# q of batches 5 to 7 transposed by DMA out of zero-padded token rows in SBUF; batch 0's last V product in other banks; a new order of steps

## The chip, the core and the metric

The kernel runs on one core of a Trainium2 chip. The metric is device time in microseconds (us) for one execution; lower is better. Engines are named as in the profile: PE multiplies matrices (PEld is its weight load), DVE is the vector engine, ACT the scalar engine, POOL issues the casting loads from DRAM and does a few copies, and SP issues the transposing DMAs and the stores.

## What is computed

Sliding-window attention over 8 batches, 8 heads, 576 positions and 64 channels, and behind it a two-layer network with the activation h - tanh(h):

```python
scores = scale * np.matmul(q, k.transpose(0, 1, 3, 2))      # q, k, v: (8, 8, 576, 64), scale = 1/8
mask = (rel >= 0) & (rel < 64)                              # rel = query position - key position
attn = softmax(where(mask, scores, -1e9))
x = (attn @ v) as 4608 tokens x 512
h = x @ w_in                                                # 512 -> 2048
out = (h - tanh(h)) @ w_out                                 # 2048 -> 512
```

## The kernel before

Everything is bf16 on PE with float32 accumulation. The kernel schedules nothing by itself: one long list of steps, `PLAN`, is played from left to right, each word is a step with its arguments, and each step puts its instructions at the end of its engines' queues. So the order within each engine is the order of the list, and an engine that waits holds up all that stands behind it.

**Attention.** Heads are taken in pairs; pair g = 4*batch + pr holds heads pr and pr+4, so that two heads share 128 partitions. A batch has nine windows of 64 queries. `Rp.g.i.bank` multiplies three windows of a pair (keys times zero-padded queries, line 300), `Rx` is their exp on ACT (line 305), `M.g` the mask multiply on DVE (line 393), `PP.g` the product with V for the two pairs g and g+1 (36 matmuls, line 418), `DR` and `DN` its normalization on DVE (lines 426 to 438) into `xs`, and `Y.b` two transposing DMAs on SP that carry a batch's `xs` into the token chunks `xT` (line 472). The first three batches reach `xT` by PE transposes instead (`Xp`, line 453, and the copies `Xc`). Batch 0 is done head by head, with `P.g` (line 405) and `D.g` (lines 445 to 447) for one pair at a time.

**How k and q reach their layouts.** For the early batches POOL loads rows with a cast (`lk`, `lq`, `LQ`, lines 108 and 114), DVE or ACT copies them into pair order (`ck`, `cq`), PE transposes them six pieces at a time (`Fp`, `Ep`, line 261), and ACT or DVE copies the result out of PSUM (`Fc`; `Ea` and `Eb` for the two halves of q, which leave the other half zero). From batch 3 on, k comes another way: `lr.b.i.h` (line 176) loads 128 tokens of four heads as rows of 64 numbers into a token-major tile, and `tk.b.i` (line 181) is a DMA transpose on SP from that tile into `kw`. For batches 6 and 7, q takes a third way: `LQ.b` loads the batch, `cz.g` (line 128, POOL) spreads a pair into the zeroed tile `qz`, `bo.g` (line 133, SP) writes that to DRAM, and `td.g` (line 138, SP) reads it back with a DMA transpose into `qT`, of which there are two (`NR = 2`).

**The network.** Tokens come in nine chunks of 512 columns. `H.c.m` is one block of 128 hidden units for chunk c (four matmuls 512 columns wide, line 487), `A.c.m` its tanh on ACT (line 495), `G.c.m` the subtraction on DVE (line 501), `W.c.s.part` four of the sixteen matmuls that make 128 output rows (line 526), and `O.c.s` the copy out of PSUM and the store (line 542). The last 128 rows of the last chunk are made in two column halves (line 519), `W.8.3.0` and `W.8.3.1` for half 0, `W.8.3.2` and `W.8.3.3` for half 1, with the stores `O.8.3` and `O.9.0` (line 537). `H` writes banks `(m + c) % 3` in chunks 0 and 1, and `m % 2` later; a bank is free again when its `G` has read it.

The weights are loaded by POOL: `wi.0`, `wi.1` and `wi.2` (line 189) hold hidden blocks 0 to 3, 4 to 7 and 8 to 15; `wo.0` to `wo.3` (line 197) hold the second layer. `U.n` are matmuls on a zero tile that only keep PE running. `z` clears the `qz` tiles (line 235). `LV`, `lv`, `lt` load V, and `Z.b`, `za`, `zb` copy V between partition halves.

## Time and profile before

| what | value |
|---|---|
| three runs | 313.97, 315.15 and 315.36 us, median 315.15 us |
| the profiled execution | 314.95 us, of which its instructions span 313.3 us |
| PE clock granted | 0.998 of full over the span |
| DMA issues by line 176, 160, 108 and 114 on POOL | 50, 35, 22 and 5 |
| DMA transposes on SP, lines 181, 138 and 472 | 25, 8 and 10 |
| DVE busy from 60 to 80 us | 18.02 of 20 us |
| last POOL instruction | before 200 us |

Rows of the groups give: line, engine, operation, tiles written<-read, shapes, how often | busy us, mean ns of one | idle us of the engine ahead of them, and what ended it. A mean for a matmul of 512 columns is 379 ns because neighbours overlap in the pipeline; what counts is how far apart their starts are, which the chain of waits shows (eight in 1.73 us). The chain's rows are: start in us, length in us, what, how many. The timeline's rows are: start, length, engine, line, operation, tiles, how many, and in brackets idle time of the engine ahead of it and who ended it.

### The profile page before, as it was taken

The numbers are of one execution on the slowest core, as the hardware profiler recorded it, in microseconds if no ns is written. First come the engines' busy times: TensorE is split into PE (matmuls) and PEld (weight loads), VectorE is DVE, ScalarE is ACT, GpSimd is POOL, SyncE is SP. The second block draws the span as 40 slices with busy tenths as digits, with TensorE's granted clock in tenths as the row PEclk, the third lists the DMA queues.
The fourth block names the chain that finished last, engine by engine and source line by source line (L and its number), as shares of the span: only waits on it lengthen the run. The fifth ranks groups of instructions, "written<-read, shape, count | busy, mean of one in ns | idle before, by whom it ended". The sixth has DMA issues, their size and how long they took to land.

```text
span 313.3 us, 6081 instructions
## 1 busy us (share of the span) xinstructions
PE 302.4 (97%) x2385; PEld 165.0 (53%) x2413; DVE 187.8 (60%) x327; ACT 171.2 (55%) x320; POOL 108.6 (35%) x160
## 2 busy tenths in 40 slices
PE   6988999999999999999999999999999999999995
PEld 2564565656655555555555455555554444444444
DVE  3685988699758785667556555873774534343300
ACT  3576875489866767657454536445333533433311
POOL 8990666686739442293441640000000000000000
PEclk9999999999999999999999999999999999999999
DMA  9999999999999999997999999481005110010111
GB/s 158 149 181 203 170 208 137 192 138 141 142 116 151 143 156 159 127 132 170 175 183 165 181 193 175 113 180 36 35 36 116 59 37 33 33 37 33 67 69 67
DMA packets 113133, 39.11 MB, mean 125 GB/s; under 512 B 96336, under 2 KB 107600, under 8 KB 113104
## 3 DMA queue, kind: packets, MB, share of 16 engines
q0 software_dynamic: 72064, 18.06, 67.1%
q1 hardware_dynamic: 41040, 20.65, 30.5%
q8 instruction: 19, 0.31, 0.4%
q14 instruction: 10, 0.08, 0.1%
HBM read 36.70 MB, written 11.80 MB: 155 GB/s over the span
## 4 chain that ended last, share of the span: by engine, by line
PE 87%; DMA 5%; POOL 5%; issue 1%; ACT 0%; POOLq 0%; ACTq 0%
PE ps L487 39%; PE ps L526 37%; PE ps L300 4%; PE ps L418 3%; DMA xT<-xs 3%; DMA wi<-in_moe_w_in_dram 3%; PE ps L261 2%; POOL kall L108 1%; POOL vw L160 1%; POOL qall L108 1%; PE ps L519 1%; PE ps L453 1%; POOL vw L147 0%; POOL seen L241 0%; ACT ysb L88 0%
## 5 line engine op out<-in xcount | busy, mean ns | idle before, releaser
L501 DVE TENSOR_TENSOR gT<-ps,th 128x512 bf16<-128x512 f32 x144 | 97.3, 687 | 81.9 <-ACT th L495 81.2
L487 PE MATMUL ps<-xT,wi 128*128 128x512 bf16 x576 | 141.7, 379 | 1.1 <-DMA wi<-in_moe_w_in_dram 0.7
L526 PE MATMUL ps<-w_out_sb,gT 128*128 128x512 bf16 x532 | 131.8, 379 | 1.4
L495 ACT ACTIVATE th<-ps 128x512 f32<-128x512 f32 x144 | 84.6, 597 | 77.8 <-PE ps L487 75.6
L487 PEld LDWEIGHTS <-wi 128*128 128x128 bf16 x576 | 62.0, 113 | 50.4 <-DMA wi<-in_moe_w_in_dram 0.9
L526 PEld LDWEIGHTS <-gT 128*128 128x128 bf16 x560 | 53.0, 98 | 56.9
L305 ACT ACTIVATE pt<-ps 128x384 bf16<-128x384 f32 (+2 forms) x92 | 45.8, 504 | 20.3 <-PE ps L300 19.0
L176 POOL DMA_DIRECT2D kall<-in_k_dram x50 | 37.2, 758 | 28.2 <-DMA kw<-kall 19.9
L160 POOL DMA_DIRECT2D vw<-in_v_dram x35 | 31.1, 894 | 10.8 <-PE ps L418 8.6
L88 ACT ACTIVATE ysb<-ps 128x512 f32<-128x512 f32 (+1 forms) x23 | 13.3, 579 | 28.4 <-PE ps L526 25.9
L393 DVE TENSOR_TENSOR pt<-pt,ps 128x1152 bf16<-128x1152 bf16 x28 | 20.6, 745 | 2.7 <-ACT pt L305 2.7
L300 PEld LDWEIGHTS <-kw 128*128 128x128 bf16 x180 | 14.4, 98 | 11.7 <-issue 0.3
L88 ACT ACTIVATE qt<-ps 64x576 bf16<-64x576 bf16 x30 | 19.3, 642 | 1.3 <-PE ps L300 0.3
L300 PE MATMUL ps<-qt,kw 128*128 128x128 bf16 x180 | 19.0, 219 | 0.0
L128 POOL COPY qz<-qall 96x384 bf16<-96x384 bf16 x16 | 7.6, 528 | 24.9 <-DMA qd<-qz 11.6
L438 DVE TENSOR_TENSOR xs<-ps,rcp 128x384 bf16<-128x384 f32 x28 | 14.9, 548 | 0.1
L225 PE MATMUL ps<-warm 128*128 128x512 bf16 x26 | 9.3, 496 | 2.2 <-DVE warm L206 2.1
L90 DVE COPY ysb<-ps 128x512 f32<-128x512 f32 x14 | 9.6, 685 | 3.1 <-PE ps L526 3.1
L418 PEld LDWEIGHTS <-pt 128*64 128x64 bf16 x504 | 9.2, 112 | 3.0 <-issue 1.3
L418 PE MATMUL ps<-vw,pt 128*64 128x65 bf16 x504 | 10.7, 197 | 0.0
L261 PE MATMUL ps<-ident,qb 96*128 96x96 bf16 x132 | 9.3, 206 | 1.0 <-DVE qb L90 1.0
L261 PEld LDWEIGHTS <-qb 96*128 96x128 bf16 x132 | 7.5, 97 | 4.5 <-DVE qb L90 1.9
(69 smaller groups left out, 165.4 us busy)
## 6 DMA issues: line engine op xcount, KB each, us to landing
out_dram<-ysb SPq DMA_DIRECT2D x35, 256.0 KB, 2.2
vw<-in_v_dram POOLq DMA_DIRECT2D x28, 128.0 KB, 5.3
qall<-in_q_dram POOLq DMA_DIRECT2D x5, 576.0 KB, 8.7
kall<-in_k_dram POOLq DMA_DIRECT2D x40, 64.0 KB, 4.8
qd<-qz SPq DMA_DIRECT2D x8, 288.0 KB, 3.3
w_out_sb<-in_moe_w_out_dram POOLq DMA_DIRECT2D x4, 512.0 KB, 8.4
kall<-in_k_dram POOLq DMA_DIRECT2D x11, 144.0 KB, 4.7
qall<-in_q_dram POOLq DMA_DIRECT2D x11, 144.0 KB, 4.6
```

Source lines behind the costliest of these rows:

```text
L88: nc.scalar.activation(o, i, ACT.Copy)
L160: nc.gpsimd.dma_start(out=w[:, 2 * i + 1, :, 0:D] if i < NF else w[64:128, 2 * i, :, 0:D], in_=v[b, :, 128 * i:128 * i + n].rearrange("h p ...
L176: nc.gpsimd.dma_start(out=token_rows(b)[0:c, i, :, h, :], in_=k[b, NP * h:NP * h + NP, 128 * i:128 * i + c].rearrange("r p d -> p r d"))
L261: nc.tensor.transpose(tp[:, e, :], src[:, e, :], ident[:P, :P])
L300: nc.tensor.matmul(sp[:, i], kt[:, 64 * j:64 * j + 128], qT[g % NR][:, :, 64 * j:64 * j + 64], start=first, stop=first or i == n - 1)
L305: nc.scalar.activation(PT[g % NPT][:, js[0]:js[0] + len(js), :].rearrange("p i (h t) -> p i h t", h=2), sp, ACT.Exp, scale=scale)
L393: nc.vector.tensor_tensor(p, p, mask.unsqueeze(1).to_broadcast([128, 2 * NJ, 64]), ALU.mult)
L418: nc.tensor.matmul(ps[r, bank, 65 * i:65 * i + 65], PT[(g + r2) % NPT][:, j, r], vw[b % 2][:, j, p0 + r2 + NP * h, :], start=True, stop=True)
L487: nc.tensor.matmul(hp, w_in_tile(ki, m), chunk_tile(c)[:, n.start // 64:n.stop // 64, ki % 2, 64 * (ki // 2):64 * (ki // 2) + 64], start=( ...
L495: nc.scalar.activation(th[:, n], hp, ACT.Tanh)
L501: nc.vector.tensor_tensor(gT[c][:, m, columns(s)], hp, th, ALU.subtract)
L526: nc.tensor.matmul(yp, gT[c][:, m, s * 128:(s + 1) * 128], w_out_sb[:, m, :], start=n == 1 and i == 0, stop=n == 4 and i == 3)
```

## The change

1. Batches 5, 6 and 7 get q in token rows. `Lq.b.half.i` on POOL loads 128 tokens (64 in the last) of four heads into the tile `q_rows`, where the other 64 columns of each head are zero; `tq.b.two.i` on SP transposes two pairs of these 128 tokens straight from SBUF into `qT`. There are 30 of each. `LQ.5` to `LQ.7`, all eight `cz`, `bo` and `td`, and the tiles `qz` and the DRAM buffer go away. So do the PE transposes of batch 5's q with their copies (`cq`, `Ep`, `Ea` and `Eb` of pairs 20 to 23).
2. `qT` has four pair slots in one tile instead of two tiles, so that `mq` clears four.
3. `z` clears `q_rows` (128 partitions of 5120 numbers) in one instruction, and stands in the list behind batch 1's last `Xc` instead of at the start.
4. Batch 0's last product with V (pair 2) goes to banks 0 and 1 instead of 5 and 6, and its normalization is cut into `DS.2` and two `DH.2`.
5. The last 128 output rows are cut at column 384: half 0 is the last 128 columns and half 1 the first 384.
6. The whole list of steps is in a new order. The end of it now ends `W.8.3.1`, `W.8.3.3`, `O.8.3`, `O.9.0` (before: `W.8.3.0`, `W.8.3.1`, `O.9.0`, `O.8.3`). The `U` matmuls are 26 before and 23 after; all of the 23 stand ahead of the first `H`.

```diff
-    qT = [const.tile([128, 2, S], BF16, name=f"qt{i}") for i in range(NR)]
+    q_two = const.tile([128, NP, 2, S], BF16, name="qt0")
+    qT = [q_two[:, i] for i in range(NP)]
+    q_rows = const.tile([128, NF + 1, NP, 2, 128], BF16, name="qr0")
-    qz = [const.tile([P, 2, E, 128], BF16, name=f"qz{i}") for i in range(2)]
...
-    def cast_q(g):
-
-        i = stage.pop((g, "q")).rearrange("p h (e d) -> p h e d", d=D)
-        for h in range(2):
-            nc.gpsimd.tensor_copy(qz[g % 2][:, h, :, 64 * h:64 * h + 64], i[:, h])
-
-    def bounce(g):
-
-        t = dram.tile([2, S, 128], BF16, tag="q", name="qd")
-        nc.sync.dma_start(out=t.rearrange("h (p e) c -> p h (e c)", e=E),
-                          in_=qz[g % 2].rearrange("p h e c -> p h (e c)"))
-        rows[g, "qd"] = t
-
-    def tr_dma(g):
-        nc.sync.dma_start(out=qT[g % NR].rearrange("c h s -> c (h s)"),
-                          in_=rows.pop((g, "qd")).rearrange("h s c -> (h s) c"), transpose=True)
+    def load_q_rows(b, half, i):
+
+        c = min(128, S - 128 * i)
+        nc.gpsimd.dma_start(out=q_rows[0:c, i, :, half, 64 * half:64 * half + 64],
+                            in_=q[b, NP * half:NP * half + NP, 128 * i:128 * i + c].rearrange("r p d -> p r d"))
+
+    def tr_q(b, two, i):
+
+        c = min(128, S - 128 * i)
+        nc.sync.dma_start(out=q_two[:, 2 * two:2 * two + 2, :, 128 * i:128 * i + c].rearrange("p r h c -> p (r h) c"),
+                          in_=q_rows[0:c, i, 2 * two:2 * two + 2].rearrange("p r h d -> p (r h d)"), transpose=True)
...
-    def more_zeros(i):
-        nc.vector.memset(qz[i], 0.0)
+    def more_zeros():
+        nc.vector.memset(q_rows, 0.0)
...
     def pv_banks(g):
-        return ps[:, 4:8:3, :] if g < NP and g % 2 and not BY_HEAD else ps[:, 5:7, :]
+        return ps[:, 0:2, :] if g == 2 else ps[:, 5:7, :]
...
+    def norm_sums(g):
+        ov = pv_banks(g)[:, :, 0:5 * (D + 1)].rearrange("p n (i c) -> p n i c", c=D + 1)
+        last[g] = sm_pool.tile([128, 2, 5, 1], F32, tag="rc", name="rc")
+        nc.vector.reciprocal(last[g], ov[:, :, :, D:D + 1])
+
+    def norm_half(g, n):
+        b, pr = divmod(g, NP)
+        k = 5 - n
+        ov = pv_banks(g)[:, n, 0:k * (D + 1)].rearrange("p (i c) -> p i c", c=D + 1)
+        nc.vector.tensor_tensor(xs[b % 2][:, 5 * n:5 * n + k, pr, :], ov[:, :, 0:D],
+                                last[g][:, n, 0:k].to_broadcast([128, k, D]), ALU.mult)
...
+    def last_columns(half):
+        n = 3 * d_model // 4
+        return slice(0, n) if half else slice(n, d_model)
```

Of the new order, the stretches that the prediction speaks of (loads and the first chunk; the end of chunk 0; the end of the list):

```diff
-    ... lq.4.p lk.4.p ... lq.7.p ... lv.1.1.1 P.3 wi.0 Eb.5.3.v wi.1 ... wi.2 ... lq.6.p ...
+    ... lq.7.p ... lk.4.p ... wi.0 ... ck.4.v P.3 D.3 ... Fp.4.3 P.2 DS.2 ... lk.7.p lk.6.p Xp.0.0.0.3 wi.1 DH.2.0 DH.2.1 ... lq.8.p Xc.0.1.0.3.v wi.2 ...
-    ... Xp.1.1.1.3 W.0.3.3 Xc.1.1.1.3.v Rx.9.1.4 Rp.8.1.4 O.0.2.a cq.10.a Ep.10.3 H.1.0 O.0.3.v ... G.1.0 ...
+    ... Xc.1.1.1.3.v z Ep.10.3 ck.10.v W.0.3.3 lr.5.2.1 Z.2 Rx.9.1.4 Rp.8.1.4 H.1.0 ... H.1.1 Fp.10.3 H.1.2 Rp.9.0.4 A.1.0 M.8 ... G.1.0 ... G.1.1 Fp.11.3 ... H.1.3 ...
-    ... W.8.2.3 W.8.3.2 O.8.1.a W.8.3.3 O.8.2.a W.8.3.0 W.8.3.1 O.9.0.a O.8.3.a
+    ... W.8.3.0 W.8.2.3 W.8.3.2 O.8.2.a W.8.3.1 W.8.3.3 O.8.3.a O.9.0.a
```

## The prediction

> **What bounds the kernel now.** I read the groups first, then the chain of waits, then the timeline at both ends.

> ```profile
> PE 302.4 (97%) x2385; PEld 165.0 (53%) x2413; DVE 187.8 (60%) x327; ACT 171.2 (55%) x320; POOL 108.6 (35%) x160
> ...
> L487 PE MATMUL ps<-xT,wi 128*128 128x512 bf16 x576 | 141.7, 379 | 1.1 <-DMA wi<-in_moe_w_in_dram 0.7
> L526 PE MATMUL ps<-w_out_sb,gT 128*128 128x512 bf16 x532 | 131.8, 379 | 1.4
> ```

> PE waits in all 2.5 us for its two large groups. The chain of waits tells when it begins and whether it ever stops:

> ```profile
> 17.52 8.44 DMA wi<-in_moe_w_in_dram
> 26.00 2.78 PE ps L487 x12
> ...
> 33.94 2.59 PE ps L487 x12
> ...
> 109.42 8.67 DMA xT<-xs
> ...
> 257.06 3.45 PE ps L526 x16
> ...
> 306.27 3.51 PE ps L519 x32
> ```

> Sixteen matmuls of 512 columns take 3.45 us, 0.216 us each. From the first of the network's matmuls at 26.00 us to the last at 309.8 us the PE's own work adds up, by such rows, to 282 us of the 283.8: 576 and 560 (weight loads; 28 matmul records are missing) x 0.216, line 519's 3.5, 243 score matmuls x 0.056, 504 V matmuls x 0.0215, 150 transposes x 0.043, 36 x 0.056. So after 26 us PE is full, and the time is: start of the first `H`, plus PE's work behind it, plus what PE is made to wait, plus the tail. The start and the tail:

> ```profile
> 25.01 0.56 DVE L90 COPY xT<-ps 128x512 bf16<-128x512 bf16 x2 [0.84 <-PE ps L453]
> ...
> 26.00 2.78 PE L487 MATMUL ps<-xT,wi 128*128 128x512 bf16 x12 [0.72 <-DMA wi<-in_moe_w_in_dram]
> ```

> ```profile
> 308.51 2.08 SPq L537 DMA_DIRECT2D out_dram<-ysb  x2
> 309.85 0.38 ACT L88 ACTIVATE ysb<-ps 128x256 f32<-128x256 f32 x1 [1.36 <-PE ps L519]
> ```

> The first `H` waits for `wi.0`; the last copy into `xT` was done 0.43 us sooner, at 25.57. Behind the last matmul come a copy of 256 columns and one store. The profiled execution took 314.95 us for a span of 313.3, 0.20 below the median of 315.15; the sum is made against 314.95.

> **PE's work behind the first H: -1.35 us.** Batch 5's q loses four `Ep`, each six transposes in 0.26 us (chain rows of line 261): -1.04. One warm-up matmul that stood near 76 us: -0.22. `Ep.4` moves ahead of the first `H` (-0.26), one score group moves behind it (+0.17). The copies that go with them (ten-odd on ACT and DVE of 0.35 to 0.83 us) and POOL's sixteen `cz` of 0.53 us lay beside full PE, so they are worth nothing.

> **First H: 0 (bounds -0.4 and +0.7).** POOL issues without a pause from 1.37 to 17.52 us, and 19 loads and the building of `ident`, `hide` and `seen` stand ahead of `wi.0` before and after, so `wi.0` goes at 17.5 and lands at 26.0 again. Batch 0's new banks save the last product its wait for the normalization before it, but `lk.4` is now the 19th load instead of the 18th, issued at 16.9 and landed some 4.5 us later (line 108's loads: 4.6 and 4.7 median), and `ck.4` on DVE waits for it ahead of `D.3`, `DS.2`, `DH.2` and three `Xc`: 21.6 + 0.4 + 1.05 + 0.2 + 0.9 + 1.5 = 25.65. The gain end is the copies' 25.57; the loss end a `lk.4` that takes the longest 5.3.

> **Wait for wi.2: +0.8 (0 to 1.4).** The three `wi` were issued back to back; the third, at 19.05, landed after 14.4 us (longest of its rows), at 33.5, and block 8, which needs it, began at 33.94, so the cover is 0.4. Now `lk.7`, `lk.6` and `lq.8` go between. Second and third landed at 28.5 and 33.5: 1024 KB in 5.0 us, so three loads of 144 KB push `wi.2` by 3 x 0.7 to 35.6. PE's work between first `H` and block 8 is eight blocks of 0.864, four score groups of 0.17, two `Fp` and the mask: 8.2, hence 34.2. I take the middle.

> **z in the full stretch of DVE: +0.8 (0 to 1.3).** Before, `z` was two clears at 3 us, where DVE had nothing. Now one of 2560 words stands at 60 us, where the windows view shows DVE at 18.02 of 20 us:

> ```profile
> 60.00:80.00 20.00, 19.96 (x189) 12.34 (x188) 18.02 (x32) 17.73 (x36) 13.65 (x19) 1.00 1.84 143
> ```

> Price: 768 words took 0.698 us and 576 words 0.538, 0.83 ns a word, so 2560 take 2.2 us. DVE then has `z` 2.2, `ck.10` 0.35, `Z.2` 1.49, `M.8` 0.74, and only then `G.1.0` 0.69. `Xc.1.1.1` ends at about 60.0, so `G.1.0` ends at 65.5. `H.1.3` needs its bank and would start at 64.6 (same count of PE's work). `H.1.0`'s start depends on none of it. What waits behind `H.1.3` is all of PE.

> **Tail: +0.35 (0.1 to 0.4).** PE's last two groups are the same columns. The last copy is 384 columns, between 0.38 (256) and 0.60 (512), so 0.49; the last store 192 KB, between 1.7 (128 KB) and 2.2 (256 KB). +0.11 and +0.25.

> **The new way of q: 0 (0 to +5).** POOL gives three `LQ` of 0.8 and sixteen `cz` back (10.9 us) and takes 30 `Lq` of 0.76 (22.8): it is done before 200 us in 108.6 us of work, so 12 more fit. SP gives eight `bo` of 0.53 and eight `td` of 1.28 back (14.5 us) and takes 30 transposes at `tk`'s median of 1.22 (37). That is cover that can run out, below. The transposes themselves move as much for batches 6 and 7 as before; batch 5 adds ten. The loads differ: 128-byte rows instead of 768.

> ```profile
> vw<-in_v_dram POOLq DMA_DIRECT2D x28, 128.0 KB, 5.3
> qall<-in_q_dram POOLq DMA_DIRECT2D x5, 576.0 KB, 8.7
> kall<-in_k_dram POOLq DMA_DIRECT2D x40, 64.0 KB, 4.8
> ...
> qall<-in_q_dram POOLq DMA_DIRECT2D x11, 144.0 KB, 4.6
> ```

> From 64 to 128 KB in short rows the landing grows by 0.5 us; from 144 to 576 KB in long rows by 4.1, 0.6 for each 64 KB. So a batch's q costs the same either way, about 5 us of transfer. [...]

> Sum: 314.95 - 1.35 + 0 + 0.8 + 0.8 + 0.35 = 315.5 us, 0.4 above the median. A difference under 0.5% (1.6 us) is no change here.

> **Rivals.** *Nothing new waits (25%).* `wi.2` and `z` are covered after all: POOL's loads ran ahead and `H.1.3` finds its bank free, and the first `H` follows the copies at 25.6. For it: the old order left PE not a single wait between 27 and 117 us in the chain, so such lists can be exact. Against: 33.5 against 33.94 shows how little room there was. 314.95 - 1.35 - 0.4 + 0.35 = 313.5.

> *SP runs late (15%, the slower side).* `tq.6` may not overwrite batch 5's q before its last scores, `Rp.23.2`, at 153.5 in the count of PE's work. Behind that stand twelve more transposes and a store on SP ahead of `Y.5`, which brings the tokens of chunk 5; `H.5.1` is due at 177.4.

> ```profile
> 144.09 2.86 SPq L472 DMA_TRANSPOSE xT<-xs  x2
> ...
> 168.94 4.72 SPq L472 DMA_TRANSPOSE xT<-xs  x2
> ```

> At 1.25 each plus 0.5, `Y.5` goes at 170.6 and lands 4.1 later (median): 2.7 of cover, so it decides from 1.45 us an issue. The rows show 1.43 in one place and 2.36 in another. At 1.9 (three at 114.4 us took 5.69), `Y.5` is 8.5 late and PE waits 5.7: 315.5 + 4 (a part of it caught in later queues) = 319.5. For it: SP is filled 13 deep; against: 1.22 is the median of 25.

> *Short rows slow the queue (15%).* If a short row costs by its busy time, the 13,824 extra ones load the 16 engines longer, the pipelines of `Lq` -> `tq` (one buffer each) stretch, and the last ones, `tq.7.0`, miss scores of batch 7 that come within 4 us of their place: 315.5 + 2 = 317.5. Against: the landings above.

> That the change leaves q's way as it was is excluded: the steps are in the list.

> **Numbers.** Forecast 45% at 315.5, with its own range 314 to 317 (bounds of the four terms). It holds nothing faster by 1.6 us and 2 of its 45 in slower. The first rival gives 22 of its 25 to faster, 3 to no change; SP late is all slower; short rows give 11 to slower, 4 to no change. Faster 0.22, same 0.50, slower 0.28. The range goes from 313.0, just under the first rival, to 318.6, which leaves out about half of SP late.

> **What would show it.** `wi.2` landing over 9 us behind `wi.0` and a gap at the ninth block; a clear of about 2.2 us at 60 us followed by a PE wait at `H.1.3`; the first `H` at 26.0; from 154 to 172 us SP rows back to back, with `Y.5`'s first issue at about 170.6; a last copy of 0.49 us; 24 fewer transposes on line 261. I am wrong if the first `H` moves by over 1 us, or if PE waits between 120 and 230 us add up to over 1 us.

## The result, and the profile after

The changed kernel took 318.39 us (median of 8 executions, 317.21 to 320.21); the kernel before, run beside it on the same chip, took 315.22 us (8 executions, 313.97 to 317.5). The ratio is 1.0099, with a 95% interval of 1.0076 to 1.0122: slower by one per cent, 3.2 us. The profiled execution of the changed kernel took 318.62 us for a span of 316.9.

First the page of the changed kernel: the engines' busy time, the clock granted to PE in 40 slices (tenths of full speed), and the two large groups of matmuls.

```profile
PE 304.7 (96%) x2360; PEld 165.3 (52%) x2386; DVE 188.8 (60%) x330; ACT 165.8 (52%) x307; POOL 119.7 (38%) x171
...
PEclk9977999999999999999999999999999999999999
...
L496 PE MATMUL ps<-xT,wi 128*128 128x512 bf16 x576 | 142.1, 380 | 1.7 <-DVE gT L510 1.2
L539 PE MATMUL ps<-w_out_sb,gT 128*128 128x512 bf16 x534 | 132.1, 379 | 1.4
```

Line 496 was 487 before, and line 539 was 526. PE has 27 weight loads fewer (of the matmuls some records are missing, so these are the better count) and yet 2.3 us more busy time: part of its work ran at a lower clock, in the third and fourth slice (7 tenths each). The wait of line 496 is now one for DVE (1.2 us), not for `wi`.

Where the 3.66 us of span are shows best when the span is cut at matmuls of line 496 that both lists reach in the same order: the first one, the first of `H.0.12` (the 49th), of `H.1.0` (the 65th) and of `H.2.1` (the 129th). The starts are read from the trace, the differences are mine. The lower rows are experiments, told of below. Each row is a single execution, and those of hybrid2 and late_join are the fastest of twelve, so a difference of a few tenths in one column says little.

| us | to first H | to H.0.12 | to H.1.0 | to H.2.1 | to the end | span |
|---|---|---|---|---|---|---|
| before | 26.00 | 12.35 | 23.27 | 23.50 | 228.14 | 313.26 |
| after | 28.03 | 13.28 | 23.67 | 24.89 | 227.05 | 316.92 |
| z_early | 28.40 | 13.16 | 23.42 | 23.81 | 227.18 | 315.97 |
| hybrid2 | 25.14 | 12.50 | 23.28 | 25.62 | 227.08 | 313.62 |
| late_join | 25.21 | 12.40 | 23.28 | 23.49 | 227.00 | 311.39 |

The change loses 2.03 us up to the first `H`, 1.33 in chunk 0, 1.39 between `H.1.0` and `H.2.1`, and wins 1.09 behind that: 3.66 in all.

The start, in the chain of waits of the changed kernel (start, duration, what):

```profile
11.05 5.77 DMA vw<-in_v_dram
...
16.87 0.25 PE ps L400 x4
...
20.52 0.76 DVE qt L90
...
21.57 0.84 DVE xs L442
...
22.49 0.61 ACT pt L300
...
23.14 0.51 PE ps L400 x17
...
25.03 0.53 PE ps L462 x4
...
28.23 1.09 PE ps L496 x4
```

No `wi` stands in it: `wi.0` landed at 24.53 and nobody waited for it. The chain goes through batch 0's attention instead: its V (`LV.0.4`, landed at 16.83; before, all of V was there at 13.87), `P.0` behind it, the copy `Eb.5.3` on DVE, `D.1`, the exponential `Rx.2.1.4`, `P.3`, and then all four transpositions `Xp`.

The same stretch in windows of 3.41 us (length, busy time of PE, PEld, DVE, ACT and POOL, granted clock, DMA share, GB/s), after and then before:

```profile
11.47:14.88 3.41, 2.87 (x58) 1.56 (x54) 1.22 (x2) 2.12 (x4) 3.27 (x8) 1.00 1.39 122
14.88:18.30 3.42, 2.16 (x54) 1.38 (x52) 2.71 (x5) 1.63 (x3) 3.42 (x6) 1.00 1.30 161
18.30:21.71 3.41, 3.41 (x61) 2.34 (x60) 1.67 (x5) 2.49 (x5) 3.41 (x6) 0.50 1.23 165
21.71:25.12 3.41, 2.00 (x58) 1.64 (x58) 2.79 (x7) 2.15 (x4) 1.61 (x3) 1.00 1.23 185
25.12:28.54 3.42, 3.42 (x32) 3.08 (x32) 2.37 (x8) 2.09 (x4) 1.84 (x3) 0.50 1.26 205
```

```profile
14.91:18.33 3.42, 3.16 (x93) 2.28 (x92) 2.72 (x6) 1.46 (x3) 3.42 (x6) 1.00 1.28 191
18.33:21.74 3.41, 2.78 (x63) 1.97 (x60) 2.76 (x7) 3.08 (x6) 3.41 (x6) 1.00 1.32 172
21.74:25.16 3.42, 2.58 (x50) 1.96 (x47) 2.31 (x5) 2.86 (x7) 1.68 (x3) 1.00 1.22 192
```

The clock column is what to look at: twice, behind a window in which PE was busy for 2.16 and 2.00 us, the next one was granted half the clock. Before, PE was busy for 2.58 us or more in each, and the clock stayed. The half clock does not come in every execution: of the eight, two with a mean clock of 0.999 took 317.2 and 318.0 us, three with 0.993 to 0.995 took 318.2 to 318.5, and three with 0.987 to 0.989 took 318.6 to 320.2. So a window at half clock goes with about 1 us, and without one the kernel is still 2.4 us slower; this is an estimate, since a longer wait in the start costs time by itself, and the half clock was seen behind such waits. The kernel before is not free of it either: of its 67 executions beside the experiments, 48 had a mean clock of 0.998 or more (median 314.92 us), 18 one of 0.992 to 0.995 (315.47), which is what one such window makes of 313 us, and one had 0.989.

The clear of `q_rows`, on DVE's and then PE's timeline of the changed kernel (start, duration, what; in brackets the idle time ahead of it and what ended it):

```profile
64.06 2.19 DVE L230 MEMSET qr<- 128x2560 uint32 x1 [0.48 <-issue]
...
68.00 0.76 DVE L388 TENSOR_TENSOR pt<-pt,ps 128x1152 bf16<-128x1152 bf16 x1
68.67 1.88 DVE L510 TENSOR_TENSOR gT<-ps,th 128x512 bf16<-128x512 f32 x3
```

```profile
67.99 0.42 PE L256 MATMUL ps<-ident,kb 96*128 96x96 bf16 x6
69.41 1.89 PE L496 MATMUL ps<-xT,wi 128*128 128x512 bf16 x8 [1.00 <-DVE gT L510]
```

The clear takes 2.19 us; everything on DVE comes behind it, `G.1.0` (the first of the three at 68.67) too, and PE waits 1.00 us ahead of `H.1.3`.

SP's queue behind the last scores of batch 5, and the tail, from timelines of the changed kernel:

```profile
158.97 9.05 SPq L133 DMA_TRANSPOSE qt<-qr  x7
...
178.28 3.33 SPq L481 DMA_TRANSPOSE xT<-xs  x2
```

```profile
312.33 0.28 ACT L88 ACTIVATE ysb<-ps 128x128 f32<-128x128 f32 x1 [1.15 <-PE ps L532]
312.63 1.85 SPq L550 DMA_DIRECT2D out_dram<-ysb  x2
313.63 0.49 ACT L88 ACTIVATE ysb<-ps 128x384 f32<-128x384 f32 x1 [1.02 <-PE ps L532]
```

`Y.5` (line 481) is issued at 178.3; PE waits for it at `H.5.1`, 0.29 us by its row and 0.45 by the distance of the starts, the only PE wait of that size between 120 and 230 us. Last, the new loads of q among the DMA issues (KB each, median us from issue to landing):

```profile
kall<-in_k_dram POOLq DMA_DIRECT2D x40, 64.0 KB, 5.3
...
qr<-in_q_dram POOLq DMA_DIRECT2D x24, 64.0 KB, 4.2
```

### The profile page after: what moved, and what is told of

Read it like the earlier page. It is cut to its first block, busy times and chain, and to the rows that moved or that the text cites. A ratio compares the mean times of both kernels' runs of the same rounds, so it can differ in the third digit from the quotient of the medians.

```text
span 316.9 us, 6055 instructions
## 1 busy us (share of the span) xinstructions
PE 304.7 (96%) x2360; PEld 165.3 (52%) x2386; DVE 188.8 (60%) x330; ACT 165.8 (52%) x307; POOL 119.7 (38%) x171
## 3 DMA queue, kind: packets, MB, share of 16 engines
q0 software_dynamic: 84016, 18.07, 69.4%
## 4 chain that ended last, share of the span: by engine, by line
PE 80%; DMA 5%; ACT 4%; POOL 4%; DVE 4%; issue 2%; ACTq 0%; POOLq 0%; DVEq 0%
PE ps L496 34%; PE ps L539 34%; PE ps L295 4%; PE ps L413 3%; DMA vw<-in_v_dram 2%; DMA kall<-in_k_dram 2%; DVE gT L510 2%; ACT th L504 2%; POOL vw L155 1%; PE ps L256 1%; DMA xT<-xs 1%; PE ps L532 1%; ACT pt L300 1%; PE ps L462 1%; ACT qt L88 1%
## 5 line engine op out<-in xcount | busy, mean ns | idle before, releaser
L127 POOL DMA_DIRECT2D qr<-in_q_dram x30 | 22.5, 765 | 42.7 <-DMA qt<-qr 28.9
L88 ACT ACTIVATE ysb<-ps 128x512 f32<-128x512 f32 (+2 forms) x21 | 12.1, 576 | 25.7 <-PE ps L539 23.4
L295 PEld LDWEIGHTS <-kw 128*128 128x128 bf16 x180 | 14.2, 98 | 11.6 <-issue 0.3
L88 ACT ACTIVATE qt<-ps 64x576 bf16<-64x576 bf16 x24 | 15.4, 642 | 5.6 <-PE ps L256 4.4
L90 DVE COPY ysb<-ps 128x512 f32<-128x512 f32 x16 | 10.9, 681 | 5.0 <-PE ps L539 5.0
L220 PE MATMUL ps<-warm 128*128 128x512 bf16 x23 | 8.6, 531 | 2.1 <-DVE warm L201 2.1
L295 PE MATMUL ps<-qt,kt 128*128 128x128 bf16 x72 | 8.4, 227 | 0.2 <-ACT pt L300 0.2
L256 PE MATMUL ps<-ident,qb 96*128 96x96 bf16 x108 | 8.1, 214 | 0.0
## 6 DMA issues: line engine op xcount, KB each, us to landing
vw<-in_v_dram POOLq DMA_DIRECT2D x28, 128.0 KB, 5.5
kall<-in_k_dram POOLq DMA_DIRECT2D x11, 144.0 KB, 4.7
qall<-in_q_dram POOLq DMA_DIRECT2D x11, 144.0 KB, 4.9
qall<-in_q_dram POOLq DMA_DIRECT2D x2, 576.0 KB, 9.2
```

Source lines behind the costliest of these rows:

```text
L88: nc.scalar.activation(o, i, ACT.Copy)
L127: nc.gpsimd.dma_start(out=q_rows[0:c, i, :, half, 64 * half:64 * half + 64], in_=q[b, NP * half:NP * half + NP, 128 * i:128 * i + c].rearr ...
L295: nc.tensor.matmul(sp[:, i], kt[:, 64 * j:64 * j + 128], qT[g % NP][:, :, 64 * j:64 * j + 64], start=first, stop=first or i == n - 1)
```

## The experiments

Theory after the two traces: all that the change loses, it loses ahead of 85 us, in the order of the first steps (late V, an idle PE, the half clock) and at the clear; the new way of q costs nothing. Rivals: DVE is overfull at 60 to 80 us whatever stands there; the start is long for another reason than the loads; the rest of the new order loses time too, hidden behind the late start. Every run was timed against the kernel before on the same chip; words are steps of the list.

**z_early: the clear where DVE idles.**

```diff
- ... Xc.1.1.1.3.v z Ep.10.3 ...
+ ... lq.1.p u z ck.5.a ...
```

> The clear of q_rows (z) goes right behind the clear of warm, where DVE idles from 2.0 to 5.28 us; nothing else changes. Theory A (the 2.19 us clear at 64.06 us holds up G.1.0 and with it H.1.3 on PE): the wait of 1.00 us ahead of H.1.3 disappears, the first H stays near 28.0, and the time falls by 1.0 to 1.4 us against the changed kernel: 317.0 to 317.4. Rival B (DVE is overfull from 60 to 80 us with or without the clear): PE waits as long there for another DVE step and the time stays at 318.0 to 318.6.

317.17 us, ratio 1.0055 (1.0034 to 1.0077). On PE's timeline the wait is gone:

```profile
67.98 0.42 PE L256 MATMUL ps<-ident,kb 96*128 96x96 bf16 x6
68.24 2.75 PE L496 MATMUL ps<-xT,wi 128*128 128x512 bf16 x12
```

`H.1.3` follows the transposes at once, and the stage from `H.1.0` to `H.2.1` takes 23.81 instead of 24.89 us. Theory A holds: 1.1 us by the stage, 1.2 by the medians, 1.4 by the ratios.

**v_early and v_early2: batch 0's V ahead.**

```diff
- ... LV.0.2 lq.2.p U.11 LV.0.0 lq.3.p lq.5.p i ... LV.0.3 ... h ... LV.0.1 ... lk.3.p ... LV.0.4 ...
+ ... LV.0.2 LV.0.3 lq.2.p U.11 LV.0.0 LV.0.1 LV.0.4 lq.3.p lq.5.p i ... h ... lk.3.p ...      v_early
+ ... LV.0.2 i LV.0.3 lq.3.p h LV.0.0 LV.0.1 LV.0.4 lq.2.p lq.5.p U.11 ... lk.3.p ...          v_early2
```

> The loads LV.0.3, LV.0.1 and LV.0.4 of batch 0's V go ahead of lq.3 and lq.5 on POOL's queue, so that the five of them are issued by about 7 us instead of 10.4. Theory A (the late V holds up Z.0 and P.0, PE idles at 14 to 17 us, and the granted clock falls to half behind that): the last V lands near 14, P.0 begins near 14.8 instead of 15.86 or 16.87, no half clock, the first H at 26.0 to 27.0 and the time lower by 1 to 2.5 us: 316 to 317.4. Rival B (the start is a long chain of copies and products between PE, ACT and DVE, whatever the V loads do): the first H stays within 0.4 us of 28.0 and the time at 318 to 318.6.

319.18 us, ratio 1.013 (1.0082 to 1.0178), worse than the change. V landed at 14.01, as meant, but the edit had moved three loads past `ident` on POOL, and everything on PE waits for `ident`:

```profile
10.23 0.56 PE L256 MATMUL ps<-ident,kb 96*128 96x96 bf16 x6 [2.57 <-POOL ident L197]
```

The first transposes came 2.2 us later than in the changed kernel (8.05). The experiment measured my edit, so I made it again with `ident` and `hide` kept ahead.

> As v_early, with POOL's building of ident and hide kept ahead of the loads that were moved: POOL's order becomes LV.0.2, ident, LV.0.3, lq.3, hide, LV.0.0, LV.0.1, LV.0.4, lq.2, lq.5, lk.3 (in v_early the three loads stood ahead of ident, and PE's first transpose came at 10.23 us instead of 8.05). Theory A (late V, in the new order of loads, is the cause of the late start): the last V lands before 14.2, P.0 begins near 15.0 and runs without a gap, the first H at 26.2 to 27.2, time 316.2 to 317.4. Rival B (the start's chain through ACT and DVE is as long without it): first H at 27.7 or later, time 318 or more.

318.42 us, ratio 1.01 (1.0072 to 1.0127); the first `H` at 27.93. Theory A falls: V is not what holds the start, for when it is there in time two other waits stand in its place, on PE's timeline:

```profile
19.26 0.45 PE L252 MATMUL ps<-ident,kall 96*64 96x96 bf16 x12 [1.19 <-DMA kall<-in_k_dram]
...
23.09 0.52 PE L400 MATMUL ps<-vw,pt 128*64 128x65 bf16 x20 [1.55 <-ACT pt L300]
```

The first is K of pair 2 (`lk.2`), which the new list issues at 13.9 us behind loads of batch 1 (before: 9.7). The second is `P.3`, at 23.09 against 23.14 in the changed kernel. Other traces say the same of V: with the changed kernel's order of these loads it landed at 15.33 in z_early and at 15.23 in banks instead of 16.83, and the first `H` came at 28.40 and 27.64.

**late_v: the same lateness put into the kernel before.**

```diff
- ... LV.0.2 Fp.0.2 LV.0.0 LV.0.4 Rp.1.1.4 lk.2.p ... lq.2.p ... lk.5.p ...
+ ... LV.0.2 lk.2.p lq.2.p lk.5.p LV.0.0 LV.0.4 Fp.0.2 Rp.1.1.4 ...
```

> The kernel before with one change: LV.0.0 and LV.0.4 of batch 0's V go behind lk.2, lq.2 and lk.5 on POOL's queue, some 2 us later, so that the last of V lands near 16 instead of 13.87. Theory A: Z.0 and P.0 start some 2 us later, PE idles in the start, the first H moves from 26.0 to 27.0 or later (0.4 us of the delay are covered by wi.0), in some executions the granted clock falls to half for one stretch, and the time rises by 1 to 3 us against before: 316.2 to 318.3. Rival B (the start has more slack than that): within 0.5 us of before.

317.09 us, ratio 1.0053 (1.0023 to 1.0082), executions from 315.97 to 321.12. In the profiled one, a slower one of 318.72, PE waited 2.9 us for `P.0`, was granted half the clock from 17.0 to 23.9 us, and began the first `H` at 29.90. So a late V is enough for such a loss, and v_early2 shows that taking it away is not enough to undo it.

**filler: warm-up products in the gaps.**

```diff
+ U.2 ahead of Fp.3.2, U.4 ahead of P.0, U.5 ahead of P.3
```

> Eleven more warm-up products of 512 columns (0.22 us each, results never read) stand in PE's idle time ahead of Fp.3.2, P.0 and P.3; nothing else changes. Theory A (the clock falls because PE idles at 14 to 17 and 22 to 25 us): the granted clock stays at 1.0 up to the first H in every profile, what is done at half clock today (some 3.4 us of it ahead of the first H, part of it hidden in waits) gets faster, and the time falls by 0.5 to 1.5 us: 316.9 to 317.9. Rival B (the clock falls for a reason that has nothing to do with idle PE): the half clock stays, the fillers themselves cost up to 2 us, and the time is 318.4 to 320.

320.45 us, ratio 1.0149 (1.0112 to 1.0186). The clock stayed at full from 13.2 us on (ten matmuls of line 289 took 0.32 us each time up to the first `H`; at half clock, at 20.90 us in the changed kernel, 0.45), but the first `H` slipped to 30.20. The warm-up bank 5 is one of those that `P.3` writes: `U.5` waited for the same thing as `P.3` (1.49 us, for ACT) and only then ran, 1.24 us on the path. It says that a full clock alone does not save this start; what the half clock costs it does not measure.

**banks: the V product of pair 2 back in banks 5 and 6.**

```diff
-        return ps[:, 0:2, :] if g == 2 else ps[:, 5:7, :]
+        return ps[:, 5:7, :]
- ... P.2 DS.2 ... DH.2.0 DH.2.1 ...
+ ... P.2 D.2 ...
```

> The changed kernel with batch 0's last product P.2 back in banks 5 and 6 and normalized in one piece (D.2 for DS.2, DH.2.0 and DH.2.1). P.2 then waits until D.3 has read the banks, at 24.83 us in the changed kernel, instead of running at 24.16. If the new banks shorten the start: first H later by 0.5 to 0.9 us and the time up by as much, 318.8 to 319.3. If the start is set elsewhere (by wi, or by the copies on ACT): no change, 318.0 to 318.6.

318.85 us, ratio 1.0111 (1.0082 to 1.0139), not to be told from the change. `P.2` waits 0.66 us for `D.3` as expected, but the first `H` came at 27.64, no later than the 27.93 to 28.40 of the other runs with this start. The new banks are worth at most what such runs differ by.

**d1_early and start3: the normalization ahead of the copy, and batch 0's loads ahead of batch 1's.**

```diff
- ... P.1 Rx.3.0.0 ... Eb.5.3.v ... Rp.2.1.4 D.1 Rx.2.1.4 ...
+ ... P.1 D.1 Rx.3.0.0 ... Eb.5.3.v ... Rp.2.1.4 Rx.2.1.4 ...                                    both
+ ... LV.0.2 i LV.0.3 lq.3.p h LV.0.0 LV.0.1 LV.0.4 lk.3.p lk.2.p lq.2.p lq.5.p U.11 ...         start3
```

> The changed kernel with D.1 right behind P.1, ahead of Eb.5.3 on DVE (before has it so). In the changed kernel P.1 ends at 19.8 us, but D.1 stands behind the copy Eb.5.3, which waits until 20.5 for its transposes, and ends at 22.41; Rx.2.1.4 on ACT and P.3 on PE (23.14 us) come behind it. Theory A (the new order on DVE is one cause of the late first H): D.1 done near 21.0, P.3 near 22.0, the first H at 26.8 to 27.3, time 317.0 to 317.8. Rival B (the start is held elsewhere, by lk.2 or ACT): first H within 0.4 us of 28.0, time 318 to 318.6.

319.33 us, ratio 1.013 (1.0104 to 1.0156). The profiled execution was disturbed (1107 us, PE busy for 99% of it), so there is no trace to read; the three others took 318.6 to 319.6. Not the time that theory A asked for.

> d1_early, and POOL's first loads in before's manner: LV.0.2, ident, LV.0.3, lq.3, hide, LV.0.0, LV.0.1, LV.0.4, lk.3, lk.2, lq.2, lq.5, so that all of batch 0 is issued ahead of batch 1 (but lk.5). In the changed kernel the last V of batch 0 landed at 16.83 and the K of pair 2 (lk.2) at 18.37; v_early2 mended the first, and PE then waited 1.2 us for the second at 18 to 19.3. Theory A (each of three hides the others: late V, late lk.2, D.1 behind a copy; only all three together give the time back): lk.2 lands near 15, no PE wait over 0.8 us between 15 and 23 us, first H at 25.0 to 26.2, the granted clock at 1.0 behind 14 us, time 315.6 to 316.6. Rival B (the new list of steps on ACT or PE is longer in itself): first H at 27 or later, time 317.2 or more.

317.71 us, ratio 1.0084 (1.0063 to 1.0105); first `H` at 27.97, in a profiled execution that is the slowest of the six (319.41; the others took 317.35 to 317.79), so that the others may have begun it earlier. By the time theory A falls again. With V and `lk.2` in time, Q of pair 2 (`lq.2`), which I had put behind them, is the late one, and `P.3` waits for ACT as before, on PE's timeline:

```profile
16.29 0.45 PE L252 MATMUL ps<-ident,qall 96*64 96x96 bf16 x12 [1.52 <-DMA qall<-in_q_dram]
...
23.79 0.52 PE L400 MATMUL ps<-vw,pt 128*64 128x65 bf16 x20 [0.69 <-ACT pt L300]
```

The new start as it is (also in z_early) and with something mended or undone (v_early2, banks, start3, combo) puts the first `H` between 27.64 and 28.40. Which of its steps would have to move stays open.

**hybrid and hybrid2: before's steps up to H.1.0, the changed kernel's behind it.**

```diff
- (the new list up to H.1.0, with pv_banks(2) in banks 0 and 1, DS.2 DH.2.0 DH.2.1)
+ (before's list up to H.1.0, with D.2 and banks 5 and 6; mq.2 mq.3 behind mk)
- ... lr.5.2.1 Z.2 H.1.0 ...                    hybrid2
+ ... lr.5.2.1 H.1.0 ... H.1.8 Z.2 ...          hybrid2
```

> Before's list of steps up to H.1.0 (its order of loads, its banks and its single normalization D.2 for batch 0's last product, and z and the clears of qt2 and qt3 at 3 to 6 us), then the changed kernel's remaining steps in their order: batches 5 to 7's q in the new way, the new order, the new tail. Theory A (all of the loss lies in the new start and in z; the new way of q and the rest of the new order cost nothing): first H at 26.0, no PE wait at H.1.3, and the time is before's less PE's 1.3 us: 313.4 to 314.2, faster than both. Rival B (the new way of q or the new order loses time too, hidden so far behind the late start): 315.5 or more, with PE waits between 60 and 230 us that add up to over 1.5 us.

319.75 us, ratio 1.0137 (1.0109 to 1.0166). The first `H` was at 25.98, but at the joint `Z.2` on DVE waited for batch 2's V, which before's start loads later, and held `H.1.3` up. DVE's timeline, and windows of 3.41 us around it:

```profile
65.21 0.70 DVE L161 COPY vw<-vw 64x2080 bf16<-64x2080 bf16 x1 [4.15 <-DMA vw<-in_v_dram]
```

```profile
63.94:67.36 3.42, 1.49 (x13) 0.85 (x12) 2.10 (x3) 3.15 (x7) 3.11 (x5) 1.00 1.45 102
67.36:70.77 3.41, 2.61 (x7) 0.97 (x7) 2.02 (x5) 0.60 (x1) 0.40 (x1) 0.50 1.43 179
```

A stall of 2.5 us in the full stretch was followed by a window at half clock, in which PE was busy for 2.61 us, the work of 1.3 us at full clock. So as an estimate the price is the wait and over a microsecond more.

> As hybrid, but Z.2 stands behind H.1.8, as before has it. In hybrid Z.2 stood on DVE ahead of G.1.0 and waited 4.15 us for batch 2's V, which before's start loads later; that held H.1.3 back by 2.7 us, and PE was at half clock for the next 3.4 us. Theory A (what is lost lies in the new start and in z): first H at 26.0, no PE wait over 0.5 us at H.1.3, granted clock 1.0, and before's time less PE's 1.3 us, with at most 0.9 us lost again at H.5.1: 313.6 to 314.8. Rival B (the rest of the new order is worse in itself): 315.5 or more.

316.51 us, ratio 1.0039 (1.0017 to 1.0061): between the theories. The start is back (25.14), the end is the changed kernel's (227.08), but the stage behind the joint takes 25.62 us, 2.1 more than before: PE waits of 0.2 to 0.5 us for `G`, for scores and for `Z.2`. It may be that each list of chunk 1 fits its own start; what would mend this stage was not tried.

**combo: start3, z early, and two transposes of q behind Y.5.**

```diff
- ... tq.6.1.0 H.4.9 ... DN.22.1 tq.6.1.2 ... tk.6.3 ... H.4.13 G.4.10 Y.5 Rp.25.1.4 ...
+ ... H.4.9 ... DN.22.1 ... tk.6.3 ... H.4.13 G.4.10 Y.5 tq.6.1.0 tq.6.1.2 Rp.25.1.4 ...
```

> start3, with z right behind the clear of warm, and two transposes of q that are due only behind 184 us (tq.6.1.2 and tq.6.1.0) behind Y.5 on SP instead of ahead of it. Theory A (start, z and SP's late Y.5 are separate terms that add): no wait at H.1.3 (1.0 to 1.2 us less than start3), no wait at H.5.1 (0.3 to 0.9 us less; Y.5's first issue near 175.6 less what the start gains), time 313.6 to 315.0, faster than both kernels. Rival B (DVE's full stretch from 60 to 80 us takes back what comes earlier, as in hybrid2): waits of over 2 us in all between 60 and 80 us, 315.5 to 316.5.

322.92 us, ratio 1.0263 (1.0225 to 1.03): wrong on both sides. The clear did what it did in z_early (23.75 us from `H.1.0` to `H.2.1`), but `Y.5` gained nothing and q came late. SP's timeline and PE's:

```profile
175.15 5.64 SPq L481 DMA_TRANSPOSE xT<-xs  x2
180.84 2.67 SPq L133 DMA_TRANSPOSE qt<-qr  x2
```

```profile
182.78 1.92 PE L496 MATMUL ps<-xT,wi 128*128 128x512 bf16 x8 [0.80 <-DMA xT<-xs]
188.01 0.50 PE L295 MATMUL ps<-qt,kw 128*128 128x128 bf16 x3 [3.31 <-DMA qt<-qr]
```

`Y.5` was issued 2.6 us earlier than in z_early (177.73) and landed 1 us later (182.73 against 181.75): its way took 7.6 instead of 4.0 us. What differs stands in POOL's timeline, here of z_early and then of combo:

```profile
178.11 0.74 POOL L127 DMA_DIRECT2D qr<-in_q_dram  x1 [6.98 <-DMA qt<-qr]
178.84 1.77 POOL L155 DMA_DIRECT2D vw<-in_v_dram  x2
```

```profile
170.48 1.49 POOL L127 DMA_DIRECT2D qr<-in_q_dram  x2 [5.01 <-issue]
171.95 1.78 POOL L155 DMA_DIRECT2D vw<-in_v_dram  x2
173.70 2.27 POOL L171 DMA_DIRECT2D kall<-in_k_dram  x3
```

In z_early POOL holds `Lq.7.0.2` back until `tq.6.1.2` has read its rows, and all the loads behind it too. My edit put `tq.6.1.2` behind `Lq.7.0.2` in the list, so POOL did not wait, and loads of q, V and K that z_early issues from 178 us on went out between 171 and 176 us, ahead of `Y.5` and beside it. So the edit did more than move two transposes, and the run says nothing of what the move alone is worth. By the list it does not compute the same thing either: batch 7's rows replace a part of batch 6's (heads 2 and 3, tokens 256 to 383) before they are transposed. The two that I had moved back landed at 188.0 and 188.2, and PE stood 3.3 us, with one window at half clock behind it.

**late_join: before's list up to W.1.0.3, the changed kernel's behind it.**

```diff
- (the new list up to W.1.0.3)
+ (before's list up to W.1.0.3, without the fillers behind the first H; mq.2 mq.3 behind mk)
+ LV.3.0 LV.3.4 lr.4.0.0 lr.4.1.1 lr.5.2.1 lr.5.2.0 lr.5.0.1 Lq.5.0.1
  O.1.0.v H.2.1 H.2.0 ... (the new list from here on)
```

The added line holds eight loads that the new list has issued by then and before's has not. Six loads of K (`lr`) and the copy `cq.15`, which before's list has already done, are left out of the rest.

> Before's list of steps as far as W.1.0.3 at 85 us (with its banks, its D.2, z and the clears of qt2 and qt3 at 3 to 6 us, without the one filler at 76 us), then the changed kernel's remaining steps in their order, with all of the new way of q. At this point the two lists differ only in eight loads, which follow at once. Theory A (all that the change loses, it loses ahead of 85 us: in the start and around the clear; the new way of q and the new order behind that cost nothing and save the 24 transposes): before reaches H.2.1 at 85.1, the changed kernel needs 227.0 from there to its end, so the span is 312.1 and the time 313.3 to 314.5, 0.3 to 0.6% under before. Rival B (from 85 us on the changed kernel lives on time that its late start gives to the loads of q; with PE 5 us earlier q and the tokens come late): PE waits of 1.5 us or more between 100 and 230 us, time 315.3 or more.

314.42 us against 314.99, ratio 0.9985 (0.9961 to 1.0009); the profiled execution, the fastest of twelve, took 313.1 us for a span of 311.4. Theory A holds: the median lies in its range, and PE is busy for 129.86 of the 130 us from 100 to 230. Windows of this kernel:

```profile
10.00:20.00 10.00, 9.69 (x208) 6.09 (x208) 6.56 (x12) 6.77 (x11) 9.86 (x17) 1.00 1.43 164
...
60.00:80.00 20.00, 19.88 (x213) 12.46 (x212) 17.85 (x33) 17.72 (x36) 14.14 (x19) 1.00 1.77 141
```

In the changed kernel PE was busy for 8.20 and 18.80 us in these. From `H.2.1` to the end late_join needs 227.00 us, the changed kernel 227.05, before 228.14. How far such a number moves by itself, the other traces show: ten executions with the new list behind this point (combo aside) lie between 226.64 and 227.56, and late_v, which has before's list there, needs 227.68. So what is new behind 85 us, all of the new way of q among it, costs nothing and saves some 0.8 us (227.1 against 227.9 in the mean, from two executions of the old list alone), with PE 5 us earlier as well. Of the kernels run it has the lowest median; whether it beats the kernel before by its 0.15% this measurement cannot tell.

## Why the prediction was right or wrong

The time fell into the range, at its upper end, 2.9 us above the forecast of 315.5; "no change" was the likeliest and it is slower by 1%. By its own test (wrong if the first `H` moves by over 1 us) the reasons were wrong in one place. That the time lies in the range is luck: the range reached so high for SP running late and for short rows, and neither cost the 2 us that the first `H` did.

**First H: 0, bounds -0.4 and +0.7. This step failed.** It came at 28.03, 2.03 late, and there is no bound in which that lay. I followed two ways to it, `wi.0` (which I put at 26.0; it landed at 24.53) and `lk.4` with the copies behind it, whose sum 25.65 took `D.3` as free at 22.0. `D.3` began at 23.76, because `P.3` began at 23.14. The way that decided, PE's own list from `P.0` over `P.1`, `Eb.5.3`, `D.1`, `Rx.2.1.4`, `P.3` to the four `Xp`, I had not added up at all; the new order of the loads of batch 0, which begins it, stood in the list of steps. The experiments show that the loss lies in the new start (before's start gives 25.1 to 26.0 with the new list behind it), not which step of it: late V alone can do it, and no single mending undoes it.

**What I had no term for: the clock.** I took the granted clock as 1.0 for good, since the one profile of before shows it so. In the changed kernel it is none to two windows in an execution (mean clocks of 0.999 down to 0.987), at an estimated 1 us each; in 19 of 67 executions before had a lower clock too, at some 0.5 us.

**Wait for wi.2: +0.8. Not there.** Its landing came 10.15 us behind `wi.0`, over 9 as I wrote, at 34.68. But the ninth block was not begun until 37.33, since the start was late. In its place came small waits for `G.0.0` and `Fc.7.3` (0.25 and 0.15 us on the timeline); from the first `H` to `H.0.12` the change loses 0.93.

**z: +0.8. Right, and a little small.** The clear took 2.19 us, for 2.2 forecast, and held `H.1.3` for 1.00; without it the stage is 1.08 us shorter and the time 1.2.

**PE's work: -1.35. The way right, the size not settled.** Of it 1.04, the four `Ep`, lie behind `H.2.1`. From there on the two profiles differ by 1.09, the wait at `H.5.1` and the tail included; by all traces it is some 0.8, and a single one moves by as much. What stood ahead of that point (the filler, `Ep.4`, one score group) was not measured by itself.

**Tail: +0.35. The copy right, the sum off.** The last copy took 0.49 us; from its start until its store has landed it takes 2.37 us (313.63 to 316.00), before 2.11 (309.85 to 311.96), so +0.26. But behind the landing the span ends 0.92 us later, before 1.30; from the last copy to the end the kernel needs 3.29 us instead of 3.41. I had not looked at that last piece. The kernels with the new tail behind before's start (hybrid, hybrid2, late_join) need 3.39 to 3.40 there, so the new tail by itself costs nothing; why the end is 0.1 us shorter with the new start stays open.

**The new way of q: 0. Right, for partly wrong reasons.** PE is idle for 0.87 us in all from 120 to 230 us (before 0.69), and late_join shows that there is no hidden cost. But I had `Y.5`'s first issue at 170.6, and it was 178.3: the first `tq.6` was issued at 158.97, not 153.5, since the start was late and a store of chunk 3 stood ahead, and 14 transposes of 1.34 us (I had counted 13, at 1.25) and that of another store followed. So *SP runs late* happened, at less than a tenth of its price (0.45 instead of 5.7), here because PE was late itself. In late_join PE was not: the first `tq.6` went at 153.49, as forecast, `Y.5` at 173.28, and it landed at 177.06, with `H.5.1` at 177.11. So the cover of 2.7 us that I had counted on was used up to the last tenth. In the other traces PE's row at `H.5.1` shows waits from none to 0.80 us.

**Short rows slow the queue: not seen.** The loads of 64 KB in short rows landed after 4.2 us, quicker than those of 144 KB in long rows (4.6 before, 4.9 after). The loads of K, of the same size, have rows as short and took 5.3, those of 64 KB of V 6.4 (before 8.0), so other things than the length of the rows count for more in these medians. POOL's DMA queue moved the same 18.07 MB in 84,016 packets instead of 72,064, and its packets took 69.4% of 316.9 us instead of 67.1% of 313.3, 4.6% more; but late_v, with before's packets, has 68.6% of 317.0 and z_early, with the new ones, 68.3% of 316.0, so single traces cannot tell the two apart. The 2 us that the sum of that rival put on short rows were a guess of mine that no run shows; these landings and shares are what the runs showed in their place.

**Nothing new waits: not so**; it asked that the first `H` follow at 25.6.

## What to carry to other kernels

When a list of steps is rewritten, add up the way to the first full stretch along every engine's own order, product by product, and not only the loads that ended last before; where several ways are of nearly one length, mending one by one may give nothing back, as here. Price a stall on PE with what may follow it: in the changed kernel two stretches of 3.4 us in which PE idled for 1.26 and 1.41 us were each followed by 3.41 us at half clock. Before a step is moved in a list, see what waited for it: in combo two transposes moved back let POOL's loads run ahead. And before blaming a part of a large change, join the two lists at a point where they differ in little: here a joint at 61 us brought waits of its own, and one at 85 us, with fourteen loads and a copy of difference, settled it.

## What the runs showed of the hardware

| run | window, us | PE busy, us | clock granted in the next window |
|---|---|---|---|
| combo | 184.12 to 187.53 | 0.58 | 0.50 |
| hybrid | 63.94 to 67.36 | 1.49 | 0.50 |
| late_v | 13.61 to 17.02 | 1.58 | 0.50 |
| after | 21.71 to 25.12 | 2.00 | 0.50 |
| after | 14.88 to 18.30 | 2.16 | 0.50 |
| after | 66.09 to 69.50 | 2.41 | 1.00 |
| before | 21.74 to 25.16 | 2.58 | 1.00 |
| combo | 180.70 to 184.12 | 2.62 | 1.00 |

These rows give no limit: in my count over the windows of thirteen traces up to 305 us, of the nine at full clock with PE busy for 1.77 to 2.16 us five were followed by one at half clock and four were not. Nor did the idle time lie in one piece: from 14.88 to 18.30 us of the changed kernel the single waits shown for PE were 0.69 and 0.57 us, and 1.26 us of idle time in all stood ahead of a half clock. In its profile the kernel before has no window under 2.58 us from 8 to 305 us; others of its executions had a lower clock all the same, as told above. No run here changes the clock alone, so the price of a window stays an estimate.

The other surprise was at 171 to 183 us, where a transpose by DMA landed 7.6 us after its issue (combo) instead of 4.0 (z_early). What differs is the loads that POOL had issued shortly before, and the DMA share of the windows view (packets' time, which may overlap) was 1.99 from its issue to its landing, against 0.97 in z_early. That a lighter queue would have given the 4.0 us back was not tried.
